# Letting the DMA cast and transpose q and k of batches 1 to 7 in an attention and channel-mix kernel

## The chip, the cores and the metric

The kernel runs on one core of a Trainium2 chip. The metric is device time in microseconds (us) of one execution. The kernel before takes 289.46 us (median of 2 runs, 289.22 to 289.69). The span of a profile, from first to last instruction, is about 2 us shorter than the time of the same run. Engines, by what these kernels use them for: PE multiplies matrices, ACT does activations and copies out of PSUM, DVE does elementwise work, POOL does casts and issues DMAs that change the type, SP issues the other DMAs.

## The reference, cut to what matters

```python
# q, k, v: (batch 8, heads 8, seq 576, head_dim 64), f32
scores = q @ k.T / 8                       # per batch and head
rel    = i - j
scores = where(0 <= rel < 128, scores - slope[h] * |rel|, -1e9)
x      = softmax(scores) @ v               # heads side by side: (8, 576, 512)
xk, xr = token-shift mixes of x and x of the position before
out    = sigmoid(xr @ w_r) * (relu(xk @ w_k) ** 2 @ w_v)
```

The kernel works on one pair of heads of one batch at a time (4 pairs in a batch, 32 in all). The score matmuls contract over head_dim. Both kernels feed them q and k in bf16 with head_dim on the partitions (64 partitions: `64*128 64x256` in the traces), while q and k lie in memory in f32 with the sequence in rows: so they transpose and cast them. That preparation is what the change is about.

## The kernel before

```python
def load_qk(it):                 # one head pair, f32, from SP
    ld = ldp.tile([128, 2 * NB, D], FP32)                  # q in rows 0-63, k in 64-127
    for i, src in enumerate((q, k)):
        nc.sync.dma_start(out=ld[64*i:64*i+64] ..., in_=src[b, 2*g:2*g+2] "h (p n) d -> p h (n d)")

def cast(it):                    # f32 -> bf16, on POOL (first four pairs: DVE)
    pool_cast(cs, ld)
    pool_cast(vs[...], vd)       # v of the pair, for the second matmul

def transp(it, half):            # 9 PE transposes of a pair in two halves, then ACT out of PSUM
    for n in range(n0, n1):
        nc.tensor.transpose(tp[...], cs[:, n], ident)      # tp: one PSUM buffer
    nc.scalar.copy(out=qk[...], in_=tp[...])

...                              # cut: scores, softmax, av, MLP "units"
for it in range(G, NIT + 1):     # G = 4 pairs in a batch, NIT = 32
    b, g = divmod(it, G)
    load_qk(it + 4); load_v(it + 4)
    scores(it, 0); scores(it, 1)
    run_units(...)               # matmuls of the MLP, and stores of its results from SP
    outT(it - 1, 0, NJ)
    transp(it + 1, 0); cast(it + 2)
    av(it, 0, NJ)
    transp(it + 1, 1)
    ...                          # cut: more run_units between these
```

The program gives PE, SP and POOL their instructions in the order written here. The MLP of two finished batches is cut into units that `run_units` puts between the attention steps.

The softmax here doesn't subtract the row's maximum and nothing guards it: scores larger than these inputs give would overflow.

## Time and profile before

| first scores of batch | 1 | 3 | 7 | end of span |
|---|---|---|---|---|
| before, us | 50.3 | 109.4 | 230.1 | 288.2 |

The start of a batch is read from PE's timeline: the first score matmul of its first pair. So the start takes 50 us; each of batches 1 to 6 takes 30.0 us ((230.1 - 50.3) / 6).

The page of the kernel before. First the busy time of each engine, its share of the span and its instructions, then the chain of waits that ended last, as shares of the span:

```profile
PE 240.5 (83%) x2192; PEld 143.2 (50%) x2192; DVE 203.8 (71%) x389; ACT 192.6 (67%) x313; POOL 74.0 (26%) x132
...
PE 58%; ACT 19%; DVE 7%; DMA 7%; issue 5%; SPq 2%; ACTq 0%; DVEq 0%
```

PE leads the chain of waits. The windows view of four batches (3 to 6) shows the stage itself. The columns are: window, its length, busy time of PE, PEld (weight loads), DVE, ACT and POOL with instruction counts, granted PE clock, mean busy share of the 16 DMA engines, GB/s:

```profile
109.00:137.00 28.00, 25.74 (x249) 14.44 (x248) 22.25 (x39) 22.17 (x33) 7.95 (x12) 1.00 0.66 141
137.00:169.00 32.00, 30.62 (x295) 18.67 (x296) 26.20 (x50) 23.89 (x42) 9.59 (x13) 1.00 0.80 174
169.00:198.00 29.00, 26.48 (x252) 14.90 (x252) 23.05 (x40) 21.92 (x32) 8.08 (x13) 1.00 0.69 147
198.00:230.00 32.00, 29.65 (x289) 18.38 (x288) 25.66 (x49) 23.73 (x42) 8.72 (x13) 1.00 0.70 155
```

PE is busy 91 to 96% of these windows, DVE 79 to 82%. A change that relieves PE and ACT can gain, but DVE is close behind. The groups that the change removes (all but the first 36 transposes and the copies of batch 0), with count, busy time and mean of one in ns:

```profile
L105 POOL TENSOR_SCALAR cs<-ld 128x1152 bf16<-128x1152 f32 x28 | 33.1, 1184 | 134.2 <-PE tp L145 74.8
...
L145 PE MATMUL tp<-ident,cs 128*128 128x128 bf16 x288 | 29.4, 235 | 22.7 <-DVE cs L118 9.3
...
L148 ACT COPY qk_94<-tp 128x640 bf16<-128x640 bf16 (+1 forms) x14 | 10.4, 746 | 6.6 <-PE tp L145 6.4
```

### The profile page before, as it was taken

To read this page: it belongs to the slowest core of one execution; us is meant where nothing else is said; L and a number is where in the kernel's file an instruction comes from. 1 tells how busy PE (TensorE), PEld (TensorE's weight loads), DVE (VectorE), ACT (ScalarE), POOL (GpSimd) and SP (SyncE) were. 2 spreads that over 40 slices of the span, in tenths; PEclk is the share of its full clock that TensorE was granted. 3 is DMA by queue.
4 is the path that set the end of the run, shared out by engine and by line. 5 is a ranking of instruction groups with operands and counts; after the bars stand their busy time and mean duration, and the time that the engine had idled before them with its cause. 6 is when DMAs were issued, how large, how long until landed. Compare 5 with 4: busy or idle time off the path is not lost.

```text
span 288.2 us, 5765 instructions
## 1 busy us (share of the span) xinstructions
PE 240.5 (83%) x2192; PEld 143.2 (50%) x2192; DVE 203.8 (71%) x389; ACT 192.6 (67%) x313; POOL 74.0 (26%) x132
## 2 busy tenths in 40 slices
PE   0335697757899998989999989898999999997994
PEld 0123364545555574545565645454555645554461
DVE  1335869786687786797897767878977888775341
ACT  1874554685778686887687777877675888744350
POOL 2651244451332022232332222324322110000000
PEclk9999999795799999999999999999999999999999
DMA  7999999999329377666985594927981611021111
GB/s 163 220 193 195 198 207 190 225 200 210 57 75 221 91 176 154 151 125 141 218 195 125 148 192 122 180 70 189 240 146 73 158 39 36 0 75 73 39 73 73
DMA packets 55595, 40.75 MB, mean 141 GB/s; under 512 B 40720, under 2 KB 42256, under 8 KB 55568
## 3 DMA queue, kind: packets, MB, share of 16 engines
q1 hardware_dynamic: 53472, 37.76, 61.7%
q0 software_dynamic: 2096, 2.62, 5.4%
q8 instruction: 17, 0.28, 0.5%
q14 instruction: 10, 0.08, 0.1%
HBM read 33.56 MB, written 9.44 MB: 149 GB/s over the span
## 4 chain that ended last, share of the span: by engine, by line
PE 58%; ACT 19%; DVE 7%; DMA 7%; issue 5%; SPq 2%; ACTq 0%; DVEq 0%
PE pv L273 17%; PE pr L260 10%; PE sa L194 6%; PE tp L145 5%; PE sa L168 5%; DMA mur_sb<-in_moe_mu_r_dram 4%; ACT rl L249 3%; ACT at_104 L175 3%; DMA vd<-in_v_dram 3%; ACT xt_109 L222 2%; ACT rs L265 2%; ACT xt_110 L222 2%; DVE xk L233 2%; PE tp L215 1%; SPq L87 1%
## 5 line engine op out<-in xcount | busy, mean ns | idle before, releaser
L273 PE MATMUL pv<-wv_sb,kk 128*128 128x512 bf16 x288 | 73.2, 383 | 0.0
L105 POOL TENSOR_SCALAR cs<-ld 128x1152 bf16<-128x1152 f32 x28 | 33.1, 1184 | 134.2 <-PE tp L145 74.8
L245 PEld LDWEIGHTS <-wk_sb 128*128 128x128 bf16 x416 | 38.7, 100 | 25.9 <-issue 8.1
L145 PE MATMUL tp<-ident,cs 128*128 128x128 bf16 x288 | 29.4, 235 | 22.7 <-DVE cs L118 9.3
L145 PEld LDWEIGHTS <-cs 128*128 128x128 bf16 x288 | 22.8, 105 | 38.0 <-issue 20.4
L251 DVE TENSOR_TENSOR kk<-rl 128x256 bf16<-128x256 bf16 (+2 forms) x104 | 36.8, 377 | 6.7 <-ACT rl L249 5.4
L260 PE MATMUL pr<-wr_sb,xr 128*128 128x512 bf16 x144 | 37.9, 386 | 0.0
L273 PEld LDWEIGHTS <-kk 128*128 128x128 bf16 x288 | 25.8, 99 | 22.6 <-issue 0.5
L279 DVE SCALAR_TENSOR_TENSOR ot<-rs,pv 128x512 f32<-128x512 bf16 x36 | 24.5, 682 | 16.5 <-PE pv L273 14.7
L265 ACT ACTIVATE rs<-pr 128x512 bf16<-128x512 f32 x36 | 21.6, 600 | 21.0 <-PE pr L260 19.9
L204 DVE TENSOR_TENSOR xu<-sa,rc 128x640 bf16<-128x640 f32 (+2 forms) x36 | 27.0, 749 | 1.1
L260 PEld LDWEIGHTS <-xr 128*128 128x128 bf16 x144 | 13.1, 99 | 12.4 <-issue 0.6
L181 DVE TENSOR_TENSOR at_104<-at_104,mask 128x1024 bf16<-128x1024 bf16 x14 | 9.7, 691 | 10.5 <-ACT at_104 L175 10.5
L215 PE MATMUL tp<-ident,xu 128*128 128x128 bf16 x160 | 15.6, 226 | 1.3 <-ACT qk_98 L148 0.8
L175 ACT ACTIVATE at_104<-sa 128x1024 bf16<-128x1024 f32 x14 | 13.7, 1020 | 4.0 <-PE sa L168 3.9
L175 ACT ACTIVATE at_105<-sa 128x1024 bf16<-128x1024 f32 x14 | 13.8, 1021 | 3.7 <-PE sa L168 3.7
L181 DVE TENSOR_TENSOR at_105<-at_105,mask 128x1024 bf16<-128x1024 bf16 x14 | 10.1, 720 | 8.3 <-ACT at_105 L175 8.3
L233 DVE SCALAR_TENSOR_TENSOR xr<-dl,mur_sb,xt_109 128x576 bf16<-128x576 bf16 (+2 forms) x20 | 15.1, 754 | 0.1
L233 DVE SCALAR_TENSOR_TENSOR xk<-dl,muk_sb,xt_109 128x576 bf16<-128x576 bf16 (+2 forms) x20 | 14.7, 733 | 0.5
L181 DVE TENSOR_TENSOR at_106<-at_106,mask 128x1024 bf16<-128x1024 bf16 x12 | 8.5, 719 | 9.0 <-ACT at_106 L175 9.0
L148 ACT COPY qk_94<-tp 128x640 bf16<-128x640 bf16 (+1 forms) x14 | 10.4, 746 | 6.6 <-PE tp L145 6.4
L215 PEld LDWEIGHTS <-xu 128*128 128x128 bf16 x160 | 11.4, 100 | 6.9 <-issue 2.1
(292 smaller groups left out, 435.8 us busy)
## 6 DMA issues: line engine op xcount, KB each, us to landing
ld<-in_q_dram SPq DMA_DIRECT2D x32, 288.0 KB, 5.3
ld<-in_k_dram SPq DMA_DIRECT2D x32, 288.0 KB, 6.1
out_dram<-ot SPq DMA_DIRECT2D x36, 256.0 KB, 2.0
vd<-in_v_dram SPq DMA_DIRECT2D x64, 128.0 KB, 6.0
tl<-in_v_dram SPq DMA_DIRECT2D x8, 128.0 KB, 7.0
wk_sb<-in_moe_w_k_dram POOLq DMA_DIRECT2D x1, 1024.0 KB, 8.9
wv_sb<-in_moe_w_v_dram POOLq DMA_DIRECT2D x1, 1024.0 KB, 17.6
wr_sb<-in_moe_w_r_dram POOLq DMA_DIRECT2D x1, 512.0 KB, 11.1
```

What stands on the lines that cost most here:

```text
L105: nc.gpsimd.tensor_scalar(out=dst, in0=src, scalar1=1.0, scalar2=0.0, op0=ALU.mult, op1=ALU.add)
L145: nc.tensor.transpose(tp[:, 128 * (n - n0):128 * (n - n0) + 128], cs[:, n].rearrange("p h d -> p (h d)"), ident)
L175: nc.scalar.activation(out=ah, in_=sa, func=AF.Exp, scale=float(scale))
L181: nc.vector.tensor_tensor(out=ah, in0=ah, in1=m4, op=ALU.mult)
L204: nc.vector.tensor_tensor(out=xu[:, t0:t1].rearrange("p t h d -> p h t d"), in0=a5[:, :, :, 0:D], in1=rc[:, :, 0:nt, None].to_broadcast([1 ...
L215: nc.tensor.transpose(tp[:, 128 * t:128 * t + 128], xu[:, t].rearrange("p h d -> p (h d)"), ident)
L233: nc.vector.scalar_tensor_tensor(out=dst[:, g, S * e + c0:S * e + c1], in0=dl[:, 0:c1 - c0], scalar=mu[:, g:g + 1], in1=xp, op0=ALU.mult, ...
L245: nc.tensor.matmul(ps[:, 0:n], lhsT=wk_sb[:, po, 128 * fo:128 * fo + 128], rhs=xk[:, po, c0:c1], start=(po == 0), stop=(po == NPO - 1))
L251: nc.vector.tensor_tensor(out=kk[:, fo, c0:c1], in0=rl[:, 0:n], in1=rl[:, 0:n], op=ALU.mult)
L260: nc.tensor.matmul(pr, lhsT=xr[:, po, 128 * c:128 * c + 128], rhs=wr_sb[:, po], start=(po == 0), stop=(po == NPO - 1))
L265: nc.scalar.activation(out=rs, in_=pr, func=AF.Tanh, scale=0.5)
L273: nc.tensor.matmul(pv, lhsT=kk[:, fo, 128 * c:128 * c + 128], rhs=wv_sb[:, fo], start=(fo == 0), stop=(fo == NFO - 1))
```

## The change

The intent: free PE of 252 transposes, ACT of 56 copies and POOL of 28 casts. POOL issues 16 loads per batch that cast f32 to bf16 on the way, into one buffer `cb`. SP then issues two transposes (DMAs that transpose on the way, `DMA_TRANSPOSE`; the texts call them crossbar transposes) per batch, one for q and one for k, from `cb` into `qt`, which has two buffers. The core of the diff:

```diff
-    qk_buf = [cst.tile([128, 2, NJ * 128], BF16, name=f"qk{i}") for i in range(NBUF)]
+    qk_buf = [cst.tile([128, 2, NJ * 128], BF16, name=f"qk{i}") for i in range(G)]
+    qt_buf = [cst.tile([128, 2, G * S + 64], BF16, name=f"qt{i}") for i in range(2)]
+    cbp = ctx.enter_context(tc.tile_pool(name="cbp", bufs=1))
+    def load_qk_batch(b, h0, h1):
+        ...
+        for h in range(h0, h1):
+            for i, src in enumerate((q, k)):
+                nc.gpsimd.dma_start(
+                    out=cb[64 * i:64 * i + 64, h // 2, :, h % 2],
+                    in_=src[b, h].rearrange("(n p) d -> p n d", p=64))
+    def transp_batch(b, i):
+        ...
+        nc.sync.dma_start_transpose(
+            qt[:, i, 0:G * S].rearrange("p (n c) -> p n c", c=64),
+            cb[64 * i:64 * i + 64].rearrange("p g n h d -> p (g n h d)"))
 ...
 # the start, inside the loop over the pairs of batch 0
         if g == 3:
             load_w(wr_sb, moe_w_r)
             load_w(wv_sb, moe_w_v)
+            load_qk_batch(1, 0, H)
 ...
             cast_tail(g)
             av(g, 2, NJ)
 ...
         if g == 3:
-            transp(4, 1)
+            transp_batch(1, 0)
+            transp_batch(1, 1)
             cast(5)
 ...
     for it in range(G, NIT + 1):
         b, g = divmod(it, G)
-        load_qk(it + 4)
         load_v(it + 4)
+        if g == 3:
+            transp_batch(b + 1, 0)
+            transp_batch(b + 1, 1)
 ...
-        transp(it + 1, 0)
         cast(it + 2)
+        if g < 3:
+            load_qk_batch(b + 1, 3 * g, min(H, 3 * g + 3))
         run_units(bud * .2)
         av(it, 0, NJ)
-        run_units(bud * .15)
-        transp(it + 1, 1)
-        run_units(bud * .15)
+        run_units(bud * .3)
```

Cut: smaller pools that make room (NBUF 5 to 4, fewer load buffers, the MLP tile `kk` cut by column range), and the offsets with which `scores` reads `qt`.

More of the change, by code (lines that the diff above doesn't have):

```diff
@@ L47 @@
     EARLY = 4
-    NBUF = 5
+    NBUF = 4
     RESERVE = 3000.0
@@ L52 @@
     cst = ctx.enter_context(tc.tile_pool(name="cst", bufs=1))
-    ldp = ctx.enter_context(tc.tile_pool(name="ldp", bufs=4))
+    ldp = ctx.enter_context(tc.tile_pool(name="ldp", bufs=3))
     vdp = ctx.enter_context(tc.tile_pool(name="vdp", bufs=4))
     tlp = ctx.enter_context(tc.tile_pool(name="tlp", bufs=2))
-    csp = ctx.enter_context(tc.tile_pool(name="csp", bufs=3))
+    cbp = ctx.enter_context(tc.tile_pool(name="cbp", bufs=1))
+    csp = ctx.enter_context(tc.tile_pool(name="csp", bufs=2))
     xup = ctx.enter_context(tc.tile_pool(name="xup", bufs=3))
     mxp = ctx.enter_context(tc.tile_pool(name="mxp", bufs=2))
-    kkp = ctx.enter_context(tc.tile_pool(name="kkp", bufs=2))
+    kkp = ctx.enter_context(tc.tile_pool(name="kkp", bufs=3))
     rlp = ctx.enter_context(tc.tile_pool(name="rlp", bufs=3))
@@ L102, in load_v, with qk_of @@
                     "(j p) d -> p j d", p=128))
+    def load_qk_batch(b, h0, h1):
+        if not 1 <= b < B:
+            return
+        if h0 == 0:
+            T["cb", b] = cbp.tile([128, G, NB, 2, D], BF16, tag="cb", name="cb")
+        cb = T["cb", b]
+        for h in range(h0, h1):
[4 more added lines that the diff above has]
+    def transp_batch(b, i):
+        if not 1 <= b < B:
+            return
+        cb = T["cb", b]
+        qt = qt_buf[b % 2]
+        nc.sync.dma_start_transpose(
+            qt[:, i, 0:G * S].rearrange("p (n c) -> p n c", c=64),
+            cb[64 * i:64 * i + 64].rearrange("p g n h d -> p (g n h d)"))
+    def qk_of(it):
+        b, g = divmod(it, G)
+        if b == 0:
+            return qk_buf[g], 0
+        return qt_buf[b % 2], S * g
     def pool_cast(dst, src):
@@ L110, in cast @@
             return
-        b, g = divmod(it, G)
-        ld, vd = T.pop(("ld", it)), T.pop(("vd", it))
-        cs = csp.tile([128, NB, 2, D], BF16, tag="cs", name="cs")
-        T["cs", it] = cs
-        ldr = ld.rearrange("p (h n) d -> p h n d", h=2)
-        csr = cs.rearrange("p n h d -> p h n d")
-        if it < EARLY:
-            nc.vector.tensor_copy(out=csr, in_=ldr)
-        else:
-            pool_cast(csr, ldr)
+        vd = T.pop(("vd", it))
+        if it < G:
+            ld = T.pop(("ld", it))
+            cs = csp.tile([128, NB, 2, D], BF16, tag="cs", name="cs")
+            T["cs", it] = cs
+            nc.vector.tensor_copy(
+                out=cs.rearrange("p n h d -> p h n d"),
+                in_=ld.rearrange("p (h n) d -> p h n d", h=2))
         vs = vs_buf[it % NBUF]
@@ L138, in transp @@
         cs = T["cs", it]
-        qk = qk_buf[it % NBUF]
-        if it < NBUF and half == 0:
+        qk = qk_buf[it]
+        if half == 0:
             nc.gpsimd.memset(qk[:, 1, S:NJ * 128], 0.0)
@@ L155, in scores @@
         b, g = divmod(it, G)
-        qk = qk_buf[it % NBUF]
+        qk, o = qk_of(it)
         at = at_buf[it % NBUF]
@@ L169, in scores @@
                     sa[:, hl, c0:c0 + n],
-                    lhsT=qk[r:r + 64, 1, 128 * u:128 * u + 128],
-                    rhs=qk[r:r + 64, 0, 128 * u:128 * u + n],
+                    lhsT=qk[r:r + 64, 1, o + 128 * u:o + 128 * u + 128],
+                    rhs=qk[r:r + 64, 0, o + 128 * u:o + 128 * u + n],
                     start=True, stop=True)
@@ L238, in mm1 @@
     def mm1(P, c0, c1, fo):
-        if c0 == 0 and fo == 0:
-            T["kk", P] = kkp.tile([128, NFO, SP], BF16, tag="kk", name="kk")
-        kk, xk = T["kk", P], T["xk", P]
+        if fo == 0:
+            T["kk", P, c0] = kkp.tile([128, NFO, 512], BF16, tag="kk", name="kk")
+        kk, xk = T["kk", P, c0], T["xk", P]
         n = c1 - c0
@@ L251, in mm1 @@
         nc.vector.tensor_tensor(
-            out=kk[:, fo, c0:c1], in0=rl[:, 0:n], in1=rl[:, 0:n], op=ALU.mult)
+            out=kk[:, fo, 0:n], in0=rl[:, 0:n], in1=rl[:, 0:n], op=ALU.mult)
     of = out.rearrange("b s m -> (b s) m")
@@ L265, in mm3, with mm2 @@
         nc.scalar.activation(out=rs, in_=pr, func=AF.Tanh, scale=0.5)
-    def mm2(P, c, half):
-        kk = T["kk", P]
+    def mm2(P, c0, c, half):
+        kk = T["kk", P, c0]
+        o = 128 * c - c0
         if half == 0:
@@ L273, in mm2 @@
             nc.tensor.matmul(
-                pv, lhsT=kk[:, fo, 128 * c:128 * c + 128], rhs=wv_sb[:, fo],
+                pv, lhsT=kk[:, fo, o:o + 128], rhs=wv_sb[:, fo],
                 start=(fo == 0), stop=(fo == NFO - 1))
@@ L294, in make_dist @@
     def make_dist():
-        di = cst.tile([128, 512], I32, name="di")
+        di = otp.tile([128, 512], I32, tag="ot", name="di")
         for (c0, n) in ((0, 256), (256, 192), (448, 64)):
@@ L330, in add_units @@
             units.append((864, lambda c=c: mm3(P, c)))
-            units.append((864, lambda c=c: mm2(P, c, 0)))
-            units.append((864, lambda c=c: mm2(P, c, 1)))
+            units.append((864, lambda c=c: mm2(P, c0, c, 0)))
+            units.append((864, lambda c=c: mm2(P, c0, c, 1)))
     def left():
@@ L351 @@
     make_identity(nc, ident)
+    for i in range(2):
+        nc.gpsimd.memset(qt_buf[i][:, 1, G * S:], 0.0)
     make_dist()
@@ L357 @@
     load_mu()
-    load_qk(4)
     def prep(it):
@@ L398 @@
             if g < 3:
-                load_qk(5 + g)
                 load_v(5 + g)
@@ L403 @@
             outT(g - 1, 2, NJ)
-        if g == 2:
-            transp(4, 0)
         if g == 3:
-            transp(4, 1)
+            transp_batch(1, 0)
+            transp_batch(1, 1)
             cast(5)
```

## The prediction

> **What bounds the kernel now.** From about 50 us to 263 us it works through batches 1 to 7 at about 30 us each. In the windows view PE is busy 18 to 19.7 of every 20 us there, DVE 14.5 to 17.5, ACT 14 to 16, POOL 4 to 7; the DMA share is 0.35 to 0.82. PE has 58% of the chain of waits, ACT 19%. So the steady state is bound by PE and its hand-overs to ACT, with DVE close behind. Before 60 us the DMA share is 1.04 to 1.13: the start is bound by DMA.
>
> **What goes.** 252 of 288 PE transposes of q and k (five in a row take 0.28 us in the timeline, about 14 us in all), 56 ACT copies of 0.75 us (42 us), 28 POOL casts of 1.18 us (33 us), and waits through the one tp tile (PE on ACT xt: about 8 us). DVE keeps about 6.5 us of the 7.45 us that a head pair takes, so even if all new work were free I would expect at most 11 to 17 us.
>
> **What comes.**
> - 112 casting loads issued by POOL. The three weight loads issued so took 0.79, 0.93 and 1.29 us of POOL; my estimate is 0.95 us each, 15 us per batch.
> - Source runs of 256 B instead of 2304 B. In this trace's DMA packets a 256 B one (loads of v) takes 29 ns, a 2304 B one 160 ns. Per batch q and k go from 1024 packets (10 us of all 16 engines) to 9216 (17 us).
> - 14 crossbar transposes of 590 KB from SP. No trace shows one. [...]
>
> **The critical path.** The buffer cb has one copy, so each batch has a serial loop: transposes of batch b done, then 16 loads issued and landed, then two transposes, then the first scores. The loads need about 18 us of POOL; with v and stores the DMA engines need about 21 us. [...] 32 us, where the loop must be under about 29 us to hide. I expect PE to idle 2 to 5 us before the first scores of most batches, so that the freed PE and ACT time becomes idle time.
> The start gets worse: POOL issues 16 loads of batch 1 before the tail casts of batch 0, where DMA is full, and the first scores of batch 1 need a whole batch loaded and transposed: about 59 us instead of 50 us.
>
> **Time.** 59 + 6 x 32 + 27 for the last batch (no loads) + 25 for the end = 303 us. Range 274 to 350. Chances: faster by over 2% 0.25, within 2% 0.13, slower by over 2% 0.62.
>
> **What would show each step.** Right: groups of scores on PE with idle time ended by the DMA into qt, once per batch; POOL busy over 110 us, DMA issues its largest group; DMA share near 1 from 60 to 230 us; ACT busy down by about 42 us; first scores of batch 1 near 59 us[...]. Wrong: PE busy 19 of 20 us throughout, idle time ended by DVE.
>
> **What would make it wrong.** If a transpose lands in under 3 us and POOL issues in under 0.8 us, the loop hides: 272 to 280 us. If a transpose takes 10 us or more[...], the loop is 40 us or longer: 340 us or above.

The loop came to 32 us: the 21 us of the DMA engines and the cut terms for the landing and the transposes. Six times these 32 us stand in the 303 us.

## More of the kernel before

One more line turned out to matter. It is from the waits of SP's queue: how long it waited, how often, and the longest. A store of a result tile (L282) waits in SP's queue until DVE has made the tile:

```profile
SPq L282 <- DVE ot L279: 130.3, 27, 14.5
```

SP stands still there for 130 us of 288 us. In this kernel that is harmless: behind the stores stand only loads that are needed four pairs later.

## The result, and the profile after

The changed kernel takes 340.16 us (median of 2 runs, 340.02 to 340.30), 50.7 us more. The ratio is 1.175 (95% interval 1.170 to 1.180). All ratios here are the mean time of one kernel's fast runs over that of the other's in the same rounds, so they are not quite the ratio of the medians.

| first scores of batch | 1 | 3 | 7 | end of span |
|---|---|---|---|---|
| before, us | 50.3 | 109.4 | 230.1 | 288.2 |
| after, us | 71.2 | 135.9 | 278.9 | 337.9 |
| lost in this stage, us | 20.9 | 5.6 | 22.3 | 0.9 |

A batch from 3 to 6 now takes 35.75 us ((278.9 - 135.9) / 4) instead of 30.2 us. The page after, with the same lines as before:

```profile
PE 235.1 (70%) x1913; PEld 132.5 (39%) x1940; DVE 203.0 (60%) x389; ACT 156.5 (46%) x257; POOL 128.7 (38%) x214
...
PE 43%; DMA 26%; DVE 14%; ACT 7%; SPq 5%; issue 3%; POOL 1%; ACTq 0%; POOLq 0%; DVEq 0%
```

ACT lost 36 us of work as intended, PE only 5 us (the stretches at half speed, shown below, take back some 12 us, an estimate from seven times 1.7 us), and DMA has risen from 7% to 26% of the chain of waits. The windows of batches 3 to 6 (as before: length, PE, PEld, DVE, ACT, POOL, granted clock, DMA share, GB/s):

```profile
136.00:171.00 35.00, 25.73 (x210) 12.96 (x214) 23.48 (x40) 16.57 (x24) 18.05 (x24) 0.89 1.03 130
171.00:208.00 37.00, 29.63 (x254) 17.20 (x260) 25.18 (x49) 18.99 (x33) 16.45 (x24) 0.92 1.02 133
208.00:243.00 35.00, 26.38 (x212) 13.31 (x216) 23.62 (x41) 17.03 (x24) 16.98 (x24) 0.89 1.05 130
243.00:279.00 36.00, 28.60 (x251) 16.91 (x256) 25.19 (x48) 18.83 (x33) 17.60 (x26) 0.93 1.01 137
```

No engine is full, and the granted clock has fallen from 1.00 to about 0.9. Where the time goes is in two lines of the waits view (who waited for whom: us in total, times, longest):

```profile
PE sa L195 <- DMA qt_102<-cb: 28.4, 4, 11.0
...
PE sa L195 <- DMA qt_101<-cb: 19.9, 3, 7.3
```

Once per batch, seven times, PE waits for a transpose into `qt`. Here is one of these, at the end of batch 3. SP's timeline first (start, duration, what):

```profile
144.96 3.02 SPq L101 DMA_DIRECT2D vd<-in_v_dram  x4
158.51 0.36 SPq L310 DMA_DIRECT2D out_dram<-ot  x1
158.96 1.00 SPq L101 DMA_DIRECT2D vd<-in_v_dram  x2
160.18 7.90 SPq L123 DMA_TRANSPOSE qt_101<-cb  x2
168.18 1.40 SPq L310 DMA_DIRECT2D out_dram<-ot  x1
```

From 148 to 158.5 us SP waits in front of a store. Only then, at 160.18, can it issue the two transposes. The packets in the trace show that the last load that they need had landed at 154.6 us. For batches 3, 5, 6 and 7 the same gap was 7.5, 7.5, 5.6 and 9.0 us. The wait of SP for result tiles is as long as it was before the change (129.2 us, 26 times); now something urgent stands behind it.

Before batch 2 there was no such gap (0.1 us), and PE still waited 5.9 us. There the loop alone made the wait: `cb` has one copy, so POOL holds back the next loads until the transposes have landed. From the waits view:

```profile
POOL cb L114 <- DMA qt_102<-cb: 44.6, 3, 15.3
...
POOL cb L114 <- DMA qt_101<-cb: 24.8, 2, 13.9
```

The loads of batches 2 to 7 start 0.6 to 1.2 us after the transposes before them have landed (for batch 2: loads from 71.7 us, landed at 88.1 us, first scores at 98.7 us). So the loop of loads and transposes does run; the gap in SP's queue is added to it.

Then PE and the chain of waits at the end of batch 3 again:

```profile
159.59 1.73 PE pv L301 x8
161.32 0.86 PE pr L287 x4
162.18 0.57 PE sa L221 x18
162.75 1.83 SPq L123
...
164.76 6.11 DMA qt_101<-cb
170.87 0.05 issue
170.91 1.03 PE sa L195 x6
171.95 0.65 PE tp L242 x5
172.60 1.71 PE pv L301 x4
174.30 0.91 PE pr L287 x4
```

PE runs out of work soon after 163 us and waits until 170.91. The last four lines show a second loss. Four `pv` matmuls take 1.71 us here; eight took 1.73 us at 159.59. Five `tp` transposes take 0.65 us where 0.28 us is usual. For 3.4 us after the wait, PE runs at half speed (the windows view gives a granted clock of 0.51 from 170.9 to 174.3 us and 1.00 after it), which costs 1.7 us; read in the same way from PE's timeline, it costs 1.3 to 2.2 us after the waits of the other batches from 2 on. Half speed came after shorter and broken idle time too. In the kernel before, PE was busy 1.61 us of the 3.4 us from 48.9 us on, in pieces, and the granted clock was 0.50 from 52.3 to 55.7 us. In `shift1` no wait of PE from 190 to 252 us was over 2.6 us, and the granted clock was 0.94 over 192 to 222 us. I cut the clock records of the traces before and after, from the first record on, into steps of 3.4 us (the shortest record that the end does not cut off). There were 133 steps at full clock: all 7 in which PE was busy under 42% were followed by half clock, 4 of the 6 between 42 and 56%, and none of the 120 over 56%.

Per batch this adds up: about 6.3 us of waiting (mean of the idle time before the first scores of batches 4 to 7: 7.3, 5.7, 6.7 and 5.6 us) and 1.7 us of half speed make 8.0 us. Without them a batch would take about 27.7 us, an estimate.

### The profile page after: what moved, and what is told of

Same layout as the page of the kernel before. It is cut to its first block, busy times and chain, and to the rows that moved or that the text cites. A ratio compares the mean times of both kernels' runs of the same rounds, so it can differ in the third digit from the quotient of the medians.

```text
span 337.9 us, 5282 instructions
## 1 busy us (share of the span) xinstructions
PE 235.1 (70%) x1913; PEld 132.5 (39%) x1940; DVE 203.0 (60%) x389; ACT 156.5 (46%) x257; POOL 128.7 (38%) x214
## 4 chain that ended last, share of the span: by engine, by line
PE 43%; DMA 26%; DVE 14%; ACT 7%; SPq 5%; issue 3%; POOL 1%; ACTq 0%; POOLq 0%; DVEq 0%
PE pv L301 15%; DMA qt_102<-cb 8%; PE pr L287 7%; DMA qt_101<-cb 6%; DMA cb<-in_q_dram 6%; DMA vd<-in_v_dram 4%; PE sa L195 4%; PE sa L221 3%; SPq L123 3%; DVE kk L278 3%; DMA wr_sb<-in_moe_w_r_dram 3%; DVE xk L260 3%; PE tp L242 2%; DVE xr L260 2%; DVE xu L231 2%
## 5 line engine op out<-in xcount | busy, mean ns | idle before, releaser
L114 POOL DMA_DIRECT2D cb<-in_q_dram x56 | 43.2, 771 | 90.1 <-DMA qt_102<-cb 44.6
L114 POOL DMA_DIRECT2D cb<-in_k_dram x56 | 42.9, 767 | 8.4 <-DMA wv_sb<-in_moe_w_v_dram 6.7
L208 DVE TENSOR_TENSOR at_107<-at_107,mask 128x1024 bf16<-128x1024 bf16 x16 | 11.2, 698 | 56.9 <-ACT at_107 L202 56.9
L202 ACT ACTIVATE at_107<-sa 128x1024 bf16<-128x1024 f32 x16 | 15.6, 1020 | 58.7 <-PE sa L195 58.7
L287 PE MATMUL pr<-wr_sb,xr 128*128 128x512 bf16 x134 | 39.7, 409 | 0.7 <-issue 0.2
L301 PEld LDWEIGHTS <-kk 128*128 128x128 bf16 x288 | 27.7, 103 | 30.7 <-issue 3.8
L195 PE MATMUL sa<-qt_102 64*128 64x256 bf16 (+2 forms) x160 | 14.0, 288 | 35.4 <-DMA qt_102<-cb 28.4
L292 ACT ACTIVATE rs<-pr 128x512 bf16<-128x512 f32 x36 | 21.6, 599 | 35.1 <-PE pr L287 34.9
L307 DVE SCALAR_TENSOR_TENSOR ot<-rs,pv 128x512 f32<-128x512 bf16 x36 | 24.5, 681 | 18.6 <-PE pv L301 18.2
L195 PE MATMUL sa<-qt_101 64*128 64x256 bf16 (+2 forms) x120 | 9.5, 281 | 22.7 <-DMA qt_101<-cb 19.9
L195 PEld LDWEIGHTS <-qt_102 64*128 64x128 bf16 x160 | 6.7, 105 | 45.8 <-DMA qt_102<-cb 30.1
L202 ACT ACTIVATE at_110<-sa 128x1024 bf16<-128x1024 f32 x16 | 15.7, 1021 | 13.9 <-PE sa L195 13.9
L287 PEld LDWEIGHTS <-xr 128*128 128x128 bf16 x144 | 14.4, 107 | 17.0 <-issue 5.9
L202 ACT ACTIVATE at_108<-sa 128x1024 bf16<-128x1024 f32 x16 | 15.9, 1023 | 7.1 <-PE sa L195 7.0
L242 PE MATMUL tp<-ident,xu 128*128 128x128 bf16 x160 | 17.4, 246 | 2.5 <-DVE xu L231 1.5
L202 ACT ACTIVATE at_109<-sa 128x1024 bf16<-128x1024 f32 x16 | 16.1, 1025 | 3.5 <-PE sa L195 3.5
L230 DVE RECIPROCAL rc<-sa 128x10 f32<-128x10 f32 (+2 forms) x36 | 7.4, 204 | 16.6 <-PE sa L221 16.5
L195 PEld LDWEIGHTS <-qt_101 64*128 64x128 bf16 x120 | 5.0, 104 | 29.4 <-DMA qt_101<-cb 21.0
```

Of the source, the lines that this page charges most:

```text
L114: nc.gpsimd.dma_start(out=cb[64 * i:64 * i + 64, h // 2, :, h % 2], in_=src[b, h].rearrange("(n p) d -> p n d", p=64))
L195: nc.tensor.matmul(sa[:, hl, c0:c0 + n], lhsT=qk[r:r + 64, 1, o + 128 * u:o + 128 * u + 128], rhs=qk[r:r + 64, 0, o + 128 * u:o + 128 * u ...
L202: nc.scalar.activation(out=ah, in_=sa, func=AF.Exp, scale=float(scale))
L242: nc.tensor.transpose(tp[:, 128 * t:128 * t + 128], xu[:, t].rearrange("p h d -> p (h d)"), ident)
L287: nc.tensor.matmul(pr, lhsT=xr[:, po, 128 * c:128 * c + 128], rhs=wr_sb[:, po], start=(po == 0), stop=(po == NPO - 1))
L292: nc.scalar.activation(out=rs, in_=pr, func=AF.Tanh, scale=0.5)
```

## The experiments

The theories at this point:
- A, place in the queue: the transposes stand in SP's in-order queue behind the stores of the third pair. They start after the loads have landed and leave one pair's work of PE to cover 10.7 us.
- B, single buffer: `cb` has one copy, so loads and transposes form a loop that is longer than the compute.
- C, packets: loads in 256 B pieces fill the DMA engines (the DMA share is 1.0 in the windows above).
- D, a ceiling: even with q and k for nothing, DVE and the hand-overs keep a batch near 28 us.

"A batch" below is the mean of batches 3 to 6, from the first scores of batch 3 to those of batch 7. The first eight experiments change the kernel after the change, unless said otherwise. All results are correct, except where one is said to be wrong.

### shift1: loads and transposes one pair earlier

```diff
-        if g == 3:
+        if g == 2:
             transp_batch(b + 1, 0)
             transp_batch(b + 1, 1)
-        if g < 3:
-            load_qk_batch(b + 1, 3 * g, min(H, 3 * g + 3))
+        nb, part = divmod(it + 1, G)
+        if part < 3:
+            load_qk_batch(nb + 1, 3 * part, min(H, 3 * part + 3))
# and load_qk_batch(2, 0, 3) at the end of the start
```

> The changed kernel with the casting loads of a batch on POOL and its two crossbar transposes on SP each placed one head pair earlier in the program (transposes at the start of the third pair instead of the fourth); nothing else. Theory A (SP order: the transposes stand in SP's queue behind the stores of the third pair, so they start 5 to 9 us after the loads have landed and only one pair's work of PE is left to cover 10.7 us): the idle time of PE before the first scores of a batch falls from 5.6 to 7.3 us to under 2 us, a batch takes 28 to 29 us instead of 34.6, the first batch does not change, about 305 us. Theory B (the single buffer cb makes loads and transposes a loop that is longer than the compute): the loop is the same in this order, a batch stays near 34 us and the time near 340 us. Theory C (the DMA engines are full with 256 B packets): a batch stays near 34 us too.

Measured: 309.93 us (309.13 and 310.73), ratio to before 1.068. A batch takes 30.3 us instead of 35.75 us, and PE does not wait for `qt` at all before batches 3, 5, 6 and 7 (3.0 us before batch 4; the other two of the three waits below are before batches 1 and 2). Now the transposes start as their loads land: at 147.8, 178.0 and 206.3 us for landings at 147.9, 178.2 and 206.4 us (the second transpose's loads land last). SP's timeline before batch 4, and the waits of PE in the whole run:

```profile
138.16 2.56 SPq L101 DMA_DIRECT2D vd<-in_v_dram  x4
147.78 7.69 SPq L123 DMA_TRANSPOSE qt<-cb  x2
...
PE sa L195 <- DMA qt<-cb: 18.6, 3, 11.0
```

Only the place of the instructions changed, and it was worth 30 us. Loads and transposes moved together, so the run alone does not separate their places; that the transposes' place mattered is read from the gap, which is gone. A batch is 1 to 2 us longer than A's number; the later runs say why.

### cb2_late: two copies of the buffer, same places

```diff
-    cbp = ctx.enter_context(tc.tile_pool(name="cbp", bufs=1))
+    cbp = ctx.enter_context(tc.tile_pool(name="cbp", bufs=2))
# to make room, batch 0 uses qt_buf[0] instead of qk_buf
```

> The changed kernel with two copies of cb (room made by letting batch 0 use qt's first buffer), the order of the transposes as it was. Theory B (single buffer): the loads run a batch ahead, the idle time of PE before the first scores goes, about 305 us. Theory A (SP order): the loads land earlier but the transposes still start behind the third pair's stores, PE idles as before, 335 to 342 us.

Measured: 357.31 us (355.52 and 359.10), ratio 1.231: 17 us slower than the change itself. So B alone, with the transposes left in their place, is not the cause; a second buffer with the transposes in the earlier place was not run. A's direction holds, but its number was missed, and the trace shows what was left out. The one buffer had kept loads and transposes apart. With two, POOL issues loads of the next batch just before the transposes, which then run beside them. SP's and POOL's timelines at that point:

```profile
123.81 11.27 SPq L122 DMA_TRANSPOSE qt<-cb  x2
```

```profile
120.64 0.76 POOL L113 DMA_DIRECT2D cb<-in_k_dram  x1
121.37 0.76 POOL L113 DMA_DIRECT2D cb<-in_q_dram  x1
122.09 0.78 POOL L113 DMA_DIRECT2D cb<-in_k_dram  x1
122.82 0.78 POOL L113 DMA_DIRECT2D cb<-in_q_dram  x1
123.54 0.79 POOL L113 DMA_DIRECT2D cb<-in_k_dram  x1
```

The two transposes hold SP for 11.27 us instead of 7.9 us. The same run has its own control. Before batches 2 and 7 no casting loads were in flight (before batch 2 only in the last 1.7 us), and the two transposes held SP for 8.1 and 7.8 us. Before batches 3 to 6 they were, and the two held it for 10.6 to 11.3 us and landed 15.0 to 15.8 us after the first issue. In the changed kernel, without loads beside them, it was 7.6 to 9.3 us and 10.1 to 11.0 us. PE's wait before batches 3 to 6 grew to 10.8 to 12.0 us. Whether the transposes lose time in the DMA engines or in their issue on SP was not tried.

### start: the order of the start

```diff
+            for gg in range(G):
+                cast_tail(gg)                 # POOL: before the 16 loads, not behind
             load_qk_batch(1, 0, H)
 ...
-            cast_tail(g)
             av(g, 2, NJ)
             if g < 3:
                 load_v(5 + g)
+            if g == 2:
+                transp_batch(1, 0)            # SP: before the first stores
+                transp_batch(1, 1)
```

> The changed kernel with only the start reordered: on POOL the tail casts of batch 0 stand before the 16 loads of batch 1 instead of behind them, and on SP the transposes of batch 1 stand before the first two stores. If the late start comes from these two orders, the first scores of batch 1 come at 59 to 62 us instead of 71.2 us (loads landed at 49.3 us plus 10.7 us for two transposes), a batch takes 34 to 35 us as before, 328 to 331 us. If the DMA engines alone set the start, the first scores stay near 70 us and the time near 339 us.

Measured: 326.82 us (326.08 and 327.55), ratio 1.126. The first scores of batch 1 come at 59.1 us instead of 71.2 us, as expected; a batch stays at 35.6 us. So 12.1 us of the 20.9 us lost at the start come from two queue orders. In the kernel after the change, POOL reached the tail casts of batch 0 only at 47.1 us, behind all 16 loads. The second half of batch 0 waited for them, the first two stores waited for that half, and the transposes of batch 1 stood behind those stores until 60.6 us, although their loads had landed at 49.3 us. Now they start at 48.65 us, before the stores:

```profile
48.65 7.88 SPq L123 DMA_TRANSPOSE qt<-cb  x2
56.63 1.72 SPq L310 DMA_DIRECT2D out_dram<-ot  x2
```

I put the other 8.8 us down to loading and transposing a whole batch before its first pair can start; of that, only the share of the packets was tried (`contig`, below).

### contig: the loads in long runs (wrong result)

```diff
-cb tile [128, G, NB, 2, D];  src[b, h] "(n p) d -> p n d"    # 256 B runs of source
+cb tile [128, G, 2, NB, D];  src[b, h] "(p n) d -> p n d"    # 2304 B runs
```

> Wrong result on purpose: the changed kernel with the layout of the casting loads made contiguous, so that one run is 2304 B of source and 1152 B of destination instead of 256 B and 128 B; 1024 packets a batch instead of 9216. Same bytes, same number of loads and transposes, same order. Theory A (SP order): loads land earlier but nothing that PE waits for does in the later batches, a batch stays at 33 to 35 us; the start may gain up to 5 us; 333 to 340 us. Theory C (packets fill the DMA engines): a batch falls to about 29 us, about 305 us.

Measured: 334.01 us (333.48 and 334.55), ratio 1.150. The casting loads go from 64512 packets to 7168. They land earlier after their first packet (12.9 to 15.2 us instead of 14.4 to 17.5 us, batches 3 to 7), and this buys nothing in the later batches: a batch takes 35.7 us. The transposes start 7.5, 11.9, 8.4 and 11.6 us after the landing, for batches 4 to 7. The wait behind the stores grows by what the loads save. C falls as the cause, as long as the transposes stand where they do; the start gains 3.5 us (first scores of batch 1 at 67.7 us).

### pair: eight short transposes instead of two long ones

```diff
-        nc.sync.dma_start_transpose(qt[:, i, 0:G * S] ..., cb[64 * i:64 * i + 64] ...)   # 590 KB
+        for g in range(G):
+            for i in range(2):
+                nc.sync.dma_start_transpose(
+                    qt[:, i, S * g:S * g + S] ..., cb[64 * i:64 * i + 64, g] ...)        # 147 KB
```

> The changed kernel with each batch's two transposes cut into eight, one per tensor and head pair (147 KB instead of 590 KB), in the same place of SP's queue, q and k of the first pair first; loads as they were. If the time of a transpose on SP's queue grows with its bytes (3.7 us for 590 KB), each takes about 0.9 us and the first scores need only the first two: idle time of PE before them falls from about 6 us to under 1 us, a batch to 29 to 30 us, 305 to 312 us. If a transpose has a large fixed cost (2 us or more each), eight take 16 us or more and the time is 340 us or more.

Measured: 311.56 us (309.40 and 313.71), ratio 1.079. One takes 1.2 us on SP and lands in 2.9 us (median). So the time is not in proportion to the bytes: from 1.2 us for 147 KB and 3.7 us for 590 KB I work out about 0.4 us fixed and 0.8 us per 147 KB, an estimate. Before batch 3, eight take 10.6 us instead of 7.7 us; before batches 4 to 7 they take 11.1 to 12.1 us instead of 7.7 to 9.3 us. That still pays, because the first scores need only the first two: PE waits for `qt` 17.7 us in all instead of 48.3 us, and a batch takes 31.4 us. The place has a share in this: before batches 4 to 7 the first transpose starts between 3.1 us before and 2.9 us after the last load lands, where it was 5.6 to 9.0 us after. The run does not separate the two. The expected 0.9 us each was too low, and a batch came out 1.4 us above the expected 30 us.

### copy: ordinary copies instead of transposes (wrong result)

```diff
-        nc.sync.dma_start_transpose(...)
+        for j in range(2):
+            nc.sync.dma_start(out=qt[64 * j:64 * j + 64, i, 0:G * S],
+                              in_=flat[:, G * S * j:G * S * j + G * S])
```

> Wrong result on purpose: the changed kernel with each crossbar transpose replaced by two ordinary copies inside SBUF of the same bytes in total (295 KB each), in the same place of SP's queue. It measures what the crossbar itself costs. If the wait is only a matter of place, copies of these bytes also land late and PE still idles 4 us or more per batch, 325 us or more. If the issue time of the crossbar transpose on SP (3.7 us each, one after the other) and its slow landing make the wait, the copies issue in about 1.3 us per tensor and land within 5 us of the first issue, idle time per batch is about 0 to 1 us, 303 to 312 us with the late start left in.

Measured: 317.38 us (316.71 and 318.04), ratio 1.099, between the two expectations. The four copies of a batch hold SP for 3.5 us where nothing else delays them (1.75 us per tensor; the expected 1.3 us is near two of the 0.60 us that SP's loads of 288 KB took in the kernel after), against 7.9 us for the two transposes. A copy lands in 4.4 us and a transpose in the kernel after in 6.5 us (medians). PE still waits 28.8 us for `qt` in all. A batch takes 33.5 us. So of the 7.8 us by which a batch is too long (35.75 us against 27.95 us in the run `free` below), transposes as against plain copies make 2.3 us. The rest is there with plain copies too, when they start this late.

### both: shift1 and start together

> The two reorders together: loads and transposes of a batch one head pair earlier, and the start with tail casts before the loads of batch 1 on POOL and its transposes before the first stores on SP. Theory A (placement in the in-order queues explains the slowdown): the two gains add, 310 minus 12 us, 296 to 300 us; first scores of batch 1 at 59 to 60 us, about 30 us per batch. If another shared limit (the DMA engines) stood behind both, they would not add: 304 us or more.

Measured: 295.38 us (4 runs, 294.22 to 296.92), ratio 1.022 (interval 1.013 to 1.030). The gains add. First scores of batch 1 come at 59.6 us, a batch takes 29.8 us. Its windows (columns as before) for batches 5 and 6:

```profile
181.00:208.00 27.00, 24.67 (x216) 12.57 (x216) 23.28 (x41) 17.04 (x24) 14.56 (x23) 1.00 1.25 158
208.00:238.00 30.00, 27.22 (x251) 16.14 (x252) 25.58 (x50) 19.04 (x33) 15.60 (x25) 1.00 1.23 162
```

The granted clock is 1.00 again. DVE is busy 85 to 86% of the time, PE 91%.

### both_contig: the packets once more, where they can count (wrong result)

The edits of `both` and `contig` together.

> Wrong result on purpose: the same as the run before with contiguous runs in the casting loads (1024 packets a batch instead of 9216). It asks what bounds the 30 us per batch that stay once PE no longer waits for the transposes. Theory C (DMA packets, the DMA share is 1.13 to 1.30 there): a batch falls by 2 us or more, under 286 us. Theory D (PE, DVE and ACT with their hand-overs bound it again, as before the change): a batch stays within 1 us, the start gains up to 3 us, 291 to 299 us.

Measured: 285.08 us (284.09 and 286.07), ratio 0.987. A batch takes 28.3 us instead of 29.8 us, and the first scores of batch 1 come at 55.8 us instead of 59.6 us. Neither expectation is met as it stands (C's time under 286 us is, but with 3.8 us from the start and 1.5 us per batch, where C asked for 2 us): packets are not the bound, but now that the transposes start when the loads land, they cost 1.5 us per batch. Once A is removed, B and C are what remains of the loop. In `both` PE still waited 2.9 us for `qt` before batch 4; here it does not wait from batch 3 on.

### free: q and k for nothing from batch 3 on (wrong result)

```diff
-        if not 1 <= b < B:       # in load_qk_batch and transp_batch of `both`
+        if not 1 <= b < 3:
```

> Wrong result on purpose: the kernel with both reorders, in which q and k are loaded and transposed for batches 1 and 2 alone, and later batches use what lies in the buffers. It measures the ceiling of the change: q and k for nothing from batch 3 on. Theory D (DVE with its hand-overs bounds a batch when PE and ACT are relieved, as I argued before): 27 to 28.5 us per batch against 30.0 before the change, 282 to 287 us. If PE had been the only bound, a batch would fall to 26 us or less, 275 us or less.

Measured: 288.83 us (288.66 and 288.99), ratio 1.000. A batch takes 27.95 us; the number for D was right, that for the whole time 2 us low. Two of its windows (columns as before):

```profile
147.00:177.00 30.00, 28.23 (x266) 16.81 (x269) 24.99 (x50) 19.10 (x34) 4.46 (x8) 1.00 0.30 85
177.00:207.00 30.00, 27.29 (x237) 13.81 (x237) 26.46 (x47) 18.02 (x27) 5.86 (x9) 1.00 0.30 84
```

PE, with its transposes gone, is still busy 27.3 to 28.5 us of each 30 us window, and DVE 24.7 to 26.5 us. PE is the busier of the two, so that DVE sets the 28 us, as D says, is not shown; the ceiling is. So the most that this change could gain in a batch, in this order of the program, is 2.2 us of 30.2 us, about 13 us over six batches. The late start took most of that back, and the run equals the kernel before.

### best, best_res and best5: a version that beats both

`best` uses the DMA transposes only where they can hide. Batches 0 and 1 go by PE transposes as before the change, so the start is the old one. Batches 2 to 7 go by casting loads and transposes cut by pair (`pair`), one pair earlier (`shift1`). The diff is abridged:

```diff
 def load_qk(it):                 # as before the change
+    if it >= 2 * G: return
 def cast(it), transp(it, half):  # q and k part as before the change
+    for it < 2 * G only
 def load_qk_batch, transp_batch:
-    if not 1 <= b < B: return
+    if not 2 <= b < B: return
# transposes as in `pair`, their places as in `shift1`, batches 0 and 1 in qt_buf
```

> A candidate that keeps the crossbar only where it can hide: batches 0 and 1 by PE transposes as before the change, batches 2 to 7 by casting loads and crossbar transposes, these cut by head pair (147 KB each) and placed, with their loads, one head pair earlier. Batch 0 and 1 use the qt buffers. Expected from the runs so far: first scores of batch 1 at 50 to 52 us as before, 29 to 30 us per batch, no idle time of PE before the first scores of a batch, 57 us from the first scores of batch 7 to the end: 281 to 288 us, that is 0 to 3% faster than before. If the loads and transposes disturb batch 1's old path or the DMA engines, 290 us or more.

Measured: 281.83 us (4 runs: 279.75, 278.67, 283.91, 285.18), against 289.19 us of the kernel before in the same rounds. First scores of batch 1 at 50.4 us, a batch 28.5 us, no wait of PE for `qt`. `best_res` holds back more MLP work for the start of a batch:

```diff
-    RESERVE = 3000.0
+    RESERVE = 8000.0
```

> The candidate of the run before with RESERVE 8000 instead of 3000 (more MLP matmuls are held back for the first pair of the next batch). If PE idles at the start of a batch because it has too little MLP work there now that the transposes are gone, a batch gains 0.5 us or more, 3 us or more in all; if DVE bounds that stage, no change within 1.5 us.

Measured: 282.72 us (282.41 and 283.04), a batch 28.55 us: no change against `best`. The expectation took this as the sign of a bound by DVE; it shows only that more held-back PE work does not help. Both runs are fast, with a ratio of 0.978 to the kernel before (interval 0.970 to 0.987): so one mixed version is shown to be faster than the kernel before, though not by more than 2%. `best5` repeats `best`:

> The candidate again, unchanged, for a verdict: its four runs lay between 278.7 and 285.2 us, and no interval could be given. Expected 278 to 284 us, a ratio of 0.96 to 0.985 to the kernel before, interval under 1.

Measured: 283.97 us (6 runs, 277.77 to 285.19). The runs of `best` fall on two levels, near 278.7 us (three runs, granted clock 0.988 to 0.998 over the run) and 282.1 to 285.2 us (seven runs, 0.973 to 0.981). By the rule that calls a run slow at 1.5% above the fastest, these seven are slow, and no interval for the fast ones is given. But all ten runs of `best` lie below all 18 runs of the kernel before (lowest 287.22 us). What sets the two levels was not tried. The two kept traces, one of each level (279.75 and 282.10 us), differ almost only in batch 1: it takes 21.9 us in `best`, at a granted clock of 1.00, and 24.0 us in `best5`, at 0.86.

## Why the prediction was right or wrong

The direction, slower, was right (in part by luck, below), and 340 us lay inside the range. The size was wrong: 13.5 us were predicted, 50.7 us came. Point by point:

- **What bounds the kernel, and the ceiling: right.** At most 11 to 17 us were to be gained. `free` gives 2.2 us per batch, 13 us over six.
- **The costs of the parts: nearly right.** A load's issue was estimated at 0.95 us and took 0.77 us; 256 B pieces were estimated at 29 ns and took 32 ns; the loads of a batch took about 18 us from the first issue to the last landing; two transposes took 10.7 us from the first issue to the first scores (160.18 to 170.91; 110 GB/s for their 1180 KB, an estimate from these two numbers). DMA issues are POOL's largest group, ACT lost 36 of the foreseen 42 us, and the DMA share is near 1, as foreseen.
- **The loop: the step that failed.** The prediction said: "The buffer cb has one copy, so each batch has a serial loop: transposes of batch b done, then 16 loads issued and landed, then two transposes, then the first scores." It took the transposes to start when the loads land. In the trace they start 5.6 to 9.0 us later (batches 3 to 7), because SP's queue reaches them only after the stores of the third pair. For batch 4 the sum is 18.2 us (first load issued 136.4, last landed 154.6) + 5.6 us (to 160.2) + 10.7 us (to 170.9) = 34.5 us, where 32 us were predicted. `shift1` shows that place was the cause: with the same single buffer and the same loads, 30.3 us per batch. `cb2_late` shows that a second buffer alone does not help. The single buffer still closes the loop (batch 2 above), as the prediction said.
- **Some luck in the direction.** Without the gap the measured parts make 18.2 + 10.7 = 28.9 us, inside the 29 us that the prediction itself gave as enough to hide. The prediction came to 32 us because it put the parts together 3 us too long, and so it forecast a loss per batch without the step that made most of it. `shift1`, without the gap, takes 30.3 us per batch, as the kernel before does (30.2 us). With both queue orders mended (`both`) the kernel is about 2% slower than before.
- **Idle time of PE: mis-sized.** Foreseen were 2 to 5 us per batch; 5.6 to 7.3 us came, and 1.7 us at half clock after each wait. The half clock was left out.
- **The start: mis-sized.** Foreseen were 59 us, 71.2 us came. The prediction named POOL's order (loads before the tail casts) as a cost but put no number on what follows from it: late tail casts, late stores, and transposes behind these stores. `start` removes this and gives 59.1 us.
- **The end: a slip of bookkeeping.** The prediction gave 27 + 25 = 52 us from the first scores of batch 7; before the change this stage took 58.1 us, after it 59.0 us. The same sum for the kernel before would have been 50 + 6 x 30 + 52 = 282 us, 6 us under its span: a check that was not made.

As a sum over the span of 337.9 us: start 12.2 us, six batches 15.7 us (207.7 against 192), end 7.0 us. Together 34.9 us above 303 us.

## What to carry to other kernels

When work moves to a DMA, look at what stands before it in the queue of the engine that issues it: waits that were harmless with only prefetches behind them become the critical path when something urgent stands there. Before trusting the size of a predicted loss, rebuild the time of the kernel before from the same stages and terms. A preparation that can be hidden in the steady state need not be used at the start, where nothing hides it: the mixed version keeps the old path there, and its runs lie below those of both kernels.
